# A fused attention and mixture-of-experts kernel on one core: first-layer weights in 8192-byte runs, attention steps ranked for each pair of batches

## The chip, the cores and the metric

The kernel runs on one core of a Trainium2 chip. The metric is the device time of one execution in microseconds (us). Engines are named as in the profile: PE is TensorE's matmul side, PEld its weight loads, DVE VectorE, ACT ScalarE, POOL GpSimd, SP SyncE, which here only issues DMAs. The granted clock (PEclk) is the share of full speed that TensorE's throttle allowed.

## The reference

Two parts, all in float32. The attention has 8 batches, 8 heads, 576 positions, head size 64 and 32 memory slots per head. Its output, laid out as 4608 rows of 512, goes into a softly routed mixture of 8 experts with 4 slots each.

```python
a = exp(phi - max(phi, axis=2)); a = a / (sum(a, axis=2) + 1e-9)      # (8, 8, 576, 32)
k_m = einsum('bhsm,bhsd->bhmd', a, k)                                 # over the 32 memory slots' softmax
v_m = einsum('bhsm,bhsd->bhmd', a, v)
attn = softmax(q @ k_m.T / 8)                                         # over the 32 slots
x = (attn @ v_m), transposed to (4608, 512)

logits = x @ moe_phi                                                  # (4608, 32)
d = softmax(logits, over the 4608 rows);  slot_input = d.T @ x        # (32, 512), 4 rows per expert
for e in range(8):
    slot_out[e] = maximum(slot_input[e] @ w1[e], 0) @ w2[e]           # w1 512x1024, w2 1024x512
out = softmax(logits, over the 32 slots) @ slot_out                   # (4608, 512)
```

q, k and v are 9.4 MB each, phi 4.7 MB, w1 and w2 16.8 MB each, the output 9.4 MB.

## The kernel before, in words

**Staging.** Work goes over four pairs of batches (`bp` 0 to 3, each with `g` 0 and 1) and, inside a pair, over four chunks of two heads (`c`). For a batch, `load_phi`, `load_kv` and `load_q` bring in phi (0.59 MB), k, v and q (1.18 MB each); two buffers each hold phi, the k/v pair and q.
- `shifted`: maximum over positions (DVE, L606), a turn on PE and a second maximum (L614, L621), its copy to all partitions (PE L630, ACT L641), subtraction (POOL, L648), exponential (ACT, L657).
- `summed`: the tree of sums on POOL (four additions, L669), a small product on PE (L679) and a reciprocal on DVE (L688).
- `pooled`: k_m and v_m on PE (L704, 72 products of 64x32 weights, two records each), scaled on the way out by ACT (L721, L728).
- `turned`: transposes of k_m (PE L748, ACT L762) and of v_m (L755, L771), then v_m times moe_phi (L781, L794), so that the logits come straight from the attention weights.
- `turn_q`: 32x32 transposes of q on DVE (L591), two for a batch.
- `scores`, `softmax`, `logits` for a chunk: products (PE L813), transposition out (DVE L827), maximum (L843), subtraction (POOL L848), exponential (ACT L853), sum (DVE L858), reciprocal (L867), multiplication (POOL L871), transposition (DVE L874), logits (PE L882).
- `route`: the softmax over rows within the pair and d.T @ x, through the small pooled forms. Near its end `wtb` is made by a multiply with a mask on DVE (L1065, four blocks of columns of which the mask keeps one per partition), and `sip`, the pair's share of the slots' inputs, by four products on PE (L1085, 8 records).

After the fourth pair the four shares are put together on DVE into SIM (last step L1233). The experts follow: `expert_in` (L1353, w1), `hidden` (L1371, L1380), `expert_out` and `tail_out` (L1413, w2), then the output rows (L1594), their evictions by ACT and DVE (L1570, L1571) and the stores (L1607). `slots` forms the weights of the output (L1523 and around it).

**Order.** Nothing is issued as written. Each step is handed to a planner (`Plan`) with an engine, an assumed cost, what it reads and writes, and a rank. `order` walks through time and takes the step that can begin first on its engine; among those that can begin together, the lowest rank. Ranks come from `plan.at(base, slope)` and, for the attention, from the tables `AT`: one for pair 0, one for pairs 1 and 2, one for pair 3. The nine first loads have a rank of their own, the place of their name in `FIRST`. All loads and stores go through SP's one queue. The planner's DMA rates are constants (`DMA_RATE` for 1 MB loads). Where TensorE has nothing to do at the start, up to `NWARM` warm-up matmuls (L520) are put in.

**Weights.** w1 comes in 16 loads of 1 MB, two for each expert (`load_w`); each puts two rows of 1024 floats (4096 bytes each), 128 rows apart, into a partition. Eleven of w2's 16 halves come in 1 MB loads, with four neighbouring rows of 512 in a partition (8192 bytes in one run); the last five come in 20 quarters of 256 KB, in runs of 1024 bytes, the left half of the output columns first. Weight buffers (`ws`, 2048 floats in each partition) lie over the tiles of the attention and are taken as those are done with.

Of the kernel before, what the change touches and what calls it, by code (L numbers as in the profile page):

```python
# [270 lines left out]
def kernel(  # L271
# [129 lines left out]
    wtbs = stack([2, 2, C, NS], 1)  # L401
# [35 lines left out]
    maskc_b = keep("maskc", [P, C])  # L437
# [6 lines left out]
    NWARM = 40  # L444
# [25 lines left out]
    add(DVE, 3.0, f, r=[ident_b], w=[maskhp_b, maskc_b, rep_b, ones_b])  # L470

# [26 lines left out]
    DMA_RATE, IN_RATE, HALF_RATE, SPREAD = 412e3, 386e3, 350e3, 1.0  # L498
# [8 lines left out]
    FIRST = ["phi0.0", "phi1.0", "mphi", "q0.0", "k0.0", "v0.0", "q1.0", "k1.0", "v1.0"]  # L507
# [37 lines left out]
    class Batch:  # L545
# [146 lines left out]
        def pooled(self, u):  # L692
# [6 lines left out]
            def f(js):  # L699
                for j in js:  # L700
                    for c in range(c0, c1):
                        for a in range(2):
                            h0 = HALF * a
                            nc.tensor.matmul(  # L704
                                acc.ap[M * c: M * c + M, a, : 2 * D],
                                ph()[h0: h0 + HALF, c, j, :],
                                kv()[h0: h0 + HALF, :, c, j * D: j * D + D],
# [5 lines left out]
            for js in (range(0, 3), range(3, 6), range(6, 9)):  # L713
                add(
                    PE, (0.075 * len(js) * self.ks, 8 * len(js) * self.ks), lambda f=f, js=js: f(js),
                    r=[pt.part(u), kvt.part(u), kvt.part(self.units + u)], w=[acc], also=[kp, vm],
                )

            def f():
                for a in range(2):  # L720
                    nc.scalar.activation(  # L721
                        kp.ap[o: o + n].rearrange("p i (r x) -> p i r x", r=R)[:, :, :, HALF * a: HALF * a + Y],
                        acc.ap[o: o + n, a, :D].rearrange("p (i x) -> p i x", i=2).unsqueeze(2)
                        .to_broadcast([n, 2, R, Y]),
                        AF.Copy, scale=rs.ap[o: o + n, a: a + 1],
                    )
                for a in range(2):
                    nc.scalar.activation(  # L728
                        vm.ap[o: o + n, a], acc.ap[o: o + n, a, D: 2 * D], AF.Copy,
                        scale=rs.ap[o: o + n, a: a + 1],  # L730
                    )

            add(
                ACT, 2 * act(P) + 2 * act(D), f, r=[acc, rs.part(u)],
                w=[kp.part(u), vm.part(u)],
            )

        def turned(self, u, vpb):
            kp, vm, kd, vT, n, o, g = self.kp, self.vm, self.kd, self.vT, self.n, u * self.n, self.g
            c0, c1, ks = u * self.ks, u * self.ks + self.ks, self.ks  # L740
            tp, tv, vpp = b_m.tile(), b_m.tile(), b_m.tile()
            ii = ident[o: o + n, o: o + n]

            def f():
                x = tp.ap.rearrange("p (i c r m) -> p i c r m", i=2, c=C, r=R)
                for i in range(2):
# [7 lines left out]
                PE, (TP, 2),  # L754
                lambda: nc.tensor.transpose(  # L755
                    tv.ap[:, :n], vm.ap[o: o + n].rearrange("p a d -> p (a d)"), ii
                ),
                r=[vm.part(u), ident_b], w=[tv], also=[vT],
            )
            add(  # L760
# [6 lines left out]
                r=[tp], w=[kd.part(u)],  # L767
            )
# [225 lines left out]
    def route(bp, ex, pair, lp):  # L994
# [66 lines left out]
        if bp == NSEG - 1:  # L1061
            fill(1, FILL + 5, [wtp])
        add(
            DVE, dve(4 * C * NS),
            lambda: nc.vector.tensor_tensor(  # L1065
                wtb.ap.rearrange("p g a c n -> p (g a) c n"),
                wtp.ap[:, : 4 * NS].rearrange("p (x n) -> p x n", x=4).unsqueeze(2)
                .to_broadcast([P, 4, C, NS]),
                maskc.unsqueeze(1).unsqueeze(3).to_broadcast([P, 4, C, NS]),
                op=ALU.mult,  # L1070
            ),
            r=[wtp, maskc_b], w=[wtb],
# [9 lines left out]
        def f():  # L1082
            for a in range(2):
                for g in range(2):
                    nc.tensor.matmul(  # L1085
                        sip.ap[HALF * a: HALF * a + HALF, :P],
                        pair[g].vm.ap[:, a, :],
                        wtb.ap[:, g, a].rearrange("p c n -> p (c n)"),
                        start=(g == 0),
                        stop=(g == 1),  # L1090
                    )
# [600 lines left out]
```

## Time and profile before

| | |
|---|---|
| runs | 202.66, 202.70 and 220.46 us, median 202.7 |
| profiled execution | 202.39 us, span 200.6 us |
| granted clock, mean | 0.973 |
| bytes moved | 76.47 MB, mean 381 GB/s, 34090 packets |
| packets | 2064 under 512 B, 15888 under 2 KB, 32400 under 8 KB |
| instruction fetches (queue q8) | 20 packets, 0.33 MB |

The prediction quotes the profile. In its slices the span is cut into 40 equal parts of 5 us, and a digit is the busy share in tenths. A row of the view by stretch has, for each engine, busy us and the number of instructions, then the granted clock, the busy share of the 16 DMA engines and GB/s. A timeline row has start and length in us, engine, line, operation, tiles, count, and in brackets the idle time before it and what ended it. A group row has busy us, mean ns of one, then idle time before it and what ended most of that. A row of the waits has total us, number and longest. A row of DMA issues has count, KB each and the median us from issue to landing.

### The profile page before, as it was taken

Reading aid. Unit: us, or ns where it says so; the run is one execution under the profiler, and the core shown is the slowest. Engines: PE = TensorE matmul, PEld = TensorE weight load, DVE = VectorE, ACT = ScalarE, POOL = GpSimd, SP = SyncE. Lnnn points to the kernel's source line nnn. Section 1 sums busy time; section 2 is a strip of 40 time slices with the busy share of each in tenths; the row PEclk is TensorE's granted clock in tenths of the full one; section 3 lists DMA queues with packets and bytes.
Section 4 is the critical chain, followed back from the end, with each engine's and each line's share of the span. In section 5 each row is a group of like instructions: output and inputs, shape, how many; then the busy total and the mean of one; then the engine's idle time right before and its main releaser. Section 6 shows DMA issues by size and latency. Waiting matters only on the chain.

```text
span 200.6 us, 6083 instructions
## 1 busy us (share of the span) xinstructions
PE 172.5 (86%) x2623; PEld 111.0 (55%) x2623; DVE 134.4 (67%) x243; ACT 70.3 (35%) x188; POOL 84.3 (42%) x84
## 2 busy tenths in 40 slices
PE   7999748978699899797999789799999999999930
PEld 6777534636457387464665347464655654557520
DVE  6822640799897899999899996478990110558810
ACT  2022314546341755607463252110201123356600
POOL 7199204589992994889964276000000000000000
PEclk9999997899969999999999999999999999999995
DMA  5999999999999999999999999999999999999996
GB/s 201 362 394 395 381 384 389 381 390 379 397 379 390 389 382 396 383 391 398 404 412 401 409 408 411 408 430 418 415 418 421 378 321 329 356 331 312 398 426 279
DMA packets 34090, 76.47 MB, mean 381 GB/s; under 512 B 2064, under 2 KB 15888, under 8 KB 32400
## 3 DMA queue, kind: packets, MB, share of 16 engines
q1 hardware_dynamic: 34064, 76.09, 100.7%
q8 instruction: 20, 0.33, 0.7%
q14 instruction: 6, 0.05, 0.1%
HBM read 66.65 MB, written 9.44 MB: 379 GB/s over the span
## 4 chain that ended last, share of the span: by engine, by line
PE 34%; DMA 26%; DVE 13%; POOL 11%; issue 4%; SPq 4%; ACT 2%; POOLq 1%; DVEq 0%
DMA arena<-in_moe_w_dram 18%; DMA arena<-in_v_dram 8%; PE bank L1594 6%; PE scbank L813 6%; PE kvbank L704 5%; SPq L502 4%; PE bank L882 4%; POOL arena L848 3%; POOL arena L669 3%; POOL arena L648 3%; POOL arena L871 3%; PE bank L1010 2%; DVE arena L606 2%; DVE arena L827 2%; DVE arena L874 2%
## 5 line engine op out<-in xcount | busy, mean ns | idle before, releaser
L648 POOL TENSOR_TENSOR arena<-arena 128x1152 f32<-128x1152 f32 x8 | 21.0, 2633 | 17.6 <-ACT arena L641 15.1
L591 DVE STREAM_TRANSPOSE arena<-top 128x1152 f32<-128x1152 f32 x16 | 21.6, 1355 | 8.4 <-DMA top<-in_q_dram 8.4
L704 PE MATMUL kvbank<-arena 64*32 64x128 f32 x1152 | 21.2, 279 | 6.1 <-issue 2.9
L520 PE MATMUL kvbank<-ones 128*128 128x256 f32 x82 | 23.7, 426 | 2.4 <-ACT arena L728 1.3
L813 PE MATMUL scbank<-arena 64*64 64x288 f32 x256 | 23.8, 445 | 2.2 <-DVE arena L827 2.1
L669 POOL TENSOR_TENSOR arena<-arena 128x128 f32<-128x128 f32 (+2 forms) x32 | 23.4, 732 | 3.2 <-ACT arena L657 1.3
L704 PEld LDWEIGHTS kvbank<-arena 64*32 64x32 f32 x1152 | 16.5, 107 | 10.8 <-issue 5.9
L871 POOL TENSOR_TENSOR arena<-arena,ssm 128x576 f32<-128x576 f32 x16 | 18.3, 1155 | 9.5 <-DVE ssm L867 7.9
L848 POOL TENSOR_TENSOR arena<-arena,smx 128x576 f32<-128x576 f32 x16 | 18.4, 1153 | 7.6 <-DVE smx L843 7.6
L882 PE MATMUL bank<-arena 128*128 128x288 f32 x64 | 18.8, 425 | 1.3 <-DVE arena L874 0.8
L606 DVE TENSOR_REDUCE arena<-arena 128x128 f32<-128x1152 f32 x8 | 17.1, 2148 | 3.7 <-DMA arena<-in_phi_dram 3.6
L520 PEld LDWEIGHTS kvbank<-ones 128*128 128x128 f32 x82 | 15.9, 209 | 6.1 <-ACT arena L728 1.7
L1571 DVE COPY arena<-bank 128x256 f32<-128x256 f32 (+1 forms) x30 | 14.2, 510 | 5.9 <-PE bank L1594 5.8
L827 DVE STREAM_TRANSPOSE arena<-scbank 128x576 f32<-128x576 f32 x16 | 12.2, 765 | 5.4 <-PE scbank L813 5.4
L1594 PE MATMUL bank<-sr,cT 64*128 64x256 f32 (+1 forms) x104 | 14.7, 355 | 0.7 <-DVE arena L1571 0.6
L813 PEld LDWEIGHTS scbank<-arena 64*64 64x64 f32 x256 | 9.8, 139 | 10.1 <-DVE arena L827 3.6
L853 ACT ACTIVATE arena<-arena 128x576 f32<-128x576 f32 x16 | 11.0, 685 | 11.2 <-POOL arena L848 11.0
L882 PEld LDWEIGHTS bank<-arena 128*128 128x128 f32 x64 | 11.2, 189 | 6.4 <-issue 1.7
L1353 PE MATMUL bank<-arena,SIM 128*32 128x256 f32 x224 | 13.2, 390 | 0.4 <-DVE SIM L1233 0.4
L1594 PEld LDWEIGHTS bank<-sr,cT 64*128 64x128 f32 x104 | 9.9, 185 | 6.4 <-DVE arena L1571 4.6
L1570 ACT COPY arena<-bank 128x256 f32<-128x256 f32 (+1 forms) x24 | 10.3, 445 | 8.4 <-PE bank L1594 7.0
L874 DVE STREAM_TRANSPOSE arena<-arena 128x576 f32<-128x576 f32 x16 | 11.9, 754 | 1.5 <-POOL arena L871 1.5
(139 smaller groups left out, 249.2 us busy)
## 6 DMA issues: line engine op xcount, KB each, us to landing
arena<-in_moe_w_dram SPq DMA_DIRECT2D x25, 1024.0 KB, 14.5
top<-in_q_dram SPq DMA_DIRECT2D x8, 1152.0 KB, 12.6
arena<-in_k_dram SPq DMA_DIRECT2D x8, 1152.0 KB, 10.1
arena<-in_v_dram SPq DMA_DIRECT2D x8, 1152.0 KB, 12.5
arena<-in_moe_w_dram SPq DMA_DIRECT2D x20, 256.0 KB, 6.0
arena<-in_phi_dram SPq DMA_DIRECT2D x8, 576.0 KB, 7.2
out_dram<-arena SPq DMA_DIRECT2D x11, 384.0 KB, 3.4
out_dram<-arena SPq DMA_DIRECT2D x1, 2304.0 KB, 8.1
```

What stands on the lines that cost most here:

```text
L520: lambda: nc.tensor.matmul(warm.ap, ones, ones.unsqueeze(1).to_broadcast([P, 2, P]), start=True, stop=True,),
L591: lambda: nc.vector.transpose(qT.ap.rearrange("p (i u y) -> p u i y", i=2, y=Y), qt.ap[:, h * QT_SZ: h * QT_SZ + QT_SZ].rearrange("p (u i ...
L606: lambda: nc.vector.tensor_reduce(mx.ap[:, c0:c1], ph().rearrange("p c j m -> p c m j"), axis=AX.X, op=ALU.max),
L648: lambda: nc.gpsimd.tensor_tensor(ph(), ph(), mb.ap[:, c0:c1].unsqueeze(2).to_broadcast([P, c1 - c0, J, M]), op=ALU.subtract,),
L669: plus = lambda o, x, y: nc.gpsimd.tensor_tensor(o, x, y, op=ALU.add)
L704: nc.tensor.matmul(acc.ap[M * c: M * c + M, a, : 2 * D], ph()[h0: h0 + HALF, c, j, :], kv()[h0: h0 + HALF, :, c, j * D: j * D + D], start= ...
L813: nc.tensor.matmul(scb.ap[HALF * g: HALF * g + HALF, a, :JY], pair[g].kd.ap[h0: h0 + HALF, i, c].rearrange("p r m -> p (r m)"), pair[g].qT ...
L827: lambda: nc.vector.transpose(ex.ap[:, c * PART: (c + 1) * PART].rearrange("p (a x) -> p a x", a=2), scb.ap[:, :, :JY],),
L848: lambda: nc.gpsimd.tensor_tensor(exv(), exv(), bc(mx), op=ALU.subtract),
L871: lambda: nc.gpsimd.tensor_tensor(exv(), exv(), bc(sm), op=ALU.mult),
L882: nc.tensor.matmul(lp.ap[:, :JY], vpb.ap[:, h, :], aT.ap[:, a * JY: (a + 1) * JY], start=(h == 0), stop=(h == H - 1),)
L1594: nc.tensor.matmul(po.ap[:, : x.stop - x.start], cT[bp].ap[y: y + HALF, j // 2 * P: j // 2 * P + P], sr.ap[y: y + HALF, t, x], start=(t == 0),
```

## The change

Four things are changed together.
1. Each w1 load still brings 256 rows of an expert, but a partition now gets two neighbouring rows, 8192 bytes in one run. The rows are split so that rows 0 to 255 fill partitions 0 to 63 and rows 256 to 511 partitions 64 to 127.
2. For that the slots' inputs must lie in the same order of rows. `wtb` gets two blocks of columns (`i`) in place of four, by a mask `maski` that is the sum of the halves of `maskc`, made once at the start; `sip` is made by 16 products of 64x32 weights with every second column of v_m, in place of four of 128x64. `wtbs` takes 256 floats less in a partition.
3. The first loads come in another order, with two warm-up matmuls fewer, and the planner's rate for 1 MB loads is set from 412 to 419 GB/s.
4. `AT` has a table for each of the four pairs and ranks more steps singly: the maximum, the sums, the softmax of each chunk, the turn of q for each batch, and the v half of what was `turned` (now `turned_k` and `turned_v`). `pooled` can be split in two, for k and for v, but no pair uses it (`if bp in ()`).

```diff
-    wtbs = stack([2, 2, C, NS], 1)
+    wtbs = stack([2, 2, 2, NS], 1)
...
-    maskc_b = keep("maskc", [P, C])
+    maskc_b = keep("maskc", [P, C + 2])
+    maski_b = Tile(ap=maskc_b.ap[:, C:])
...
+    maskc = maskc[:, :C]
-    NWARM = 40
+    NWARM = 38
...
+    add(
+        DVE, 0.1,
+        lambda: nc.vector.tensor_tensor(maski_b.ap, maskc[:, :2], maskc[:, 2:], op=ALU.add),
+        r=[maskc_b], w=[maski_b],
+    )
...
-    DMA_RATE, IN_RATE, HALF_RATE, SPREAD = 412e3, 386e3, 350e3, 1.0
+    DMA_RATE, IN_RATE, HALF_RATE, SPREAD = 419e3, 386e3, 350e3, 1.0
...
-    FIRST = ["phi0.0", "phi1.0", "mphi", "q0.0", "k0.0", "v0.0", "q1.0", "k1.0", "v1.0"]
+    FIRST = [
+        "phi0.0",
+        "v0.0",
+        "k0.0",
+        "q1.0",
+        "v1.0",
+        "phi1.0",
+        "mphi",
+        "q0.0",
+        "k1.0",
+    ]
...
-        def turned(self, u, vpb):
...
+        def turned_k(self, u):
...
+        def turned_v(self, u, vpb):
...
         add(
-            DVE, dve(4 * C * NS),
+            DVE, dve(8 * NS),
             lambda: nc.vector.tensor_tensor(
-                wtb.ap.rearrange("p g a c n -> p (g a) c n"),
+                wtb.ap.rearrange("p g a i n -> p (g a) i n"),
                 wtp.ap[:, : 4 * NS].rearrange("p (x n) -> p x n", x=4).unsqueeze(2)
-                .to_broadcast([P, 4, C, NS]),
-                maskc.unsqueeze(1).unsqueeze(3).to_broadcast([P, 4, C, NS]),
+                .to_broadcast([P, 4, 2, NS]),
+                maski_b.ap.unsqueeze(1).unsqueeze(3).to_broadcast([P, 4, 2, NS]),
                 op=ALU.mult,
             ),
...
         def f():
-            for a in range(2):
+            to = sip.ap[:, :P].rearrange("p (i c n) -> p c i n", i=2, c=2)
+            for c in range(2):
                 for g in range(2):
-                    nc.tensor.matmul(
-                        sip.ap[HALF * a: HALF * a + HALF, :P],
-                        pair[g].vm.ap[:, a, :],
-                        wtb.ap[:, g, a].rearrange("p c n -> p (c n)"),
-                        start=(g == 0),
-                        stop=(g == 1),
-                    )
-
-        add(PE, (0.5, 16), f, r=[wtb, *(x.vm for x in pair)], w=[sip])
+                    for a in range(2):
+                        for y in range(2):
+                            k, x = HALF * y, HALF * y + NS * a
+                            nc.tensor.matmul(
+                                to[x: x + NS, c],
+                                pair[g].vm.ap[k: k + HALF, a, c::2],
+                                wtb.ap[k: k + HALF, g, a],
+                                start=(g == 0),
+                                stop=(g == 1),
+                                tile_position=(k, x),
+                            )
+
+        add(PE, (0.65, 64), f, r=[wtb, *(x.vm for x in pair)], w=[sip])
...
     AT = (
         dict(
...
+            phi=(-1.705, -2.946),
+            max=(-2.707, -6.465),
+            kv=(-0.702, -0.388),
+            sum=(-14.509, 1.214),
+            pool=(-13.306, 6.445),
+            vals=(15.095, 13.191),
+            q=(-2.516, -1.841),
+            turn=(5.179, 26.671, 17.592, 9.626),
+            chunk=(-1.277, -18.958, 1.909, 11.734),
+            soft=(-4.626, -2.857, -0.985, -0.647),
+            logit=(9.329, 4.84, -1.05, 5.792),
+            route=-1.016,
         ),
...
-        at = AT[(bp > 0) + (bp == NBP - 1)]
+        at = AT[bp]
...
+                plan.at(bp + at["max"][i], 8)
                 x.shifted(u)
...
+                plan.at(bp + at["sum"][i], 8)
+                x.summed(u)
                 plan.at(bp + at["pool"][i], 8)
...
+                else:
+                    x.pooled(u)
+                    x.turned_k(u)
+                    plan.at(bp + at["vals"][i], 8)
+                x.turned_v(u, vpb)
...
         for h in range(2):
-            plan.at(bp + at["turn"][h])
             for x in pair:
+                plan.at(bp + at["turn"][2 * h + x.g])
                 x.turn_q(h)
...
             scores(c, pair, ex)
+            plan.at(bp + at["soft"][c], 15)
             aT = softmax(c, ex)
...
-        load(lambda: t.ap.rearrange("p (a x) -> p a x", a=src.shape[1]), src, 1 << 20, t)
+        load(lambda: t.ap, src, 1 << 20, t)
...
-        w1v = w1[e].rearrange("(c p) f -> p c f", p=P)
-        w1b = [load_w(w1v[:, 2 * i: 2 * i + 2], wqs if e == EG else ws) for i in range(2)]
+        w1v = w1[e].rearrange("(y i x z) f -> i y x (z f)", y=2, i=2, z=2)
+        w1b = [load_w(w1v[i], wqs if e == EG else ws) for i in range(2)]
```

More of the change, by code (lines that the diff above doesn't have):

```diff
@@ new lines, in f @@
+                if y1 == 2:
+                    for a in range(2):
+                        nc.scalar.activation(
+                            vm.ap[o: o + n, a], acc.ap[o: o + n, a, D: 2 * D], AF.Copy,
+                            scale=rs.ap[o: o + n, a: a + 1],
+                        )
+            add(
+                ACT, 2 * (1 - y0) * act(P) + 2 * (y1 - 1) * act(D), f, r=[acc, rs.part(u)],
+                w=[kp.part(u), vm.part(u)][y0:y1],
+            )
+        def turned_k(self, u):
+            kp, kd, n, o = self.kp, self.kd, self.n, u * self.n
+            c0, c1 = u * self.ks, u * self.ks + self.ks
+            tp = b_m.tile()
@@ L753, in turned @@
             add(
[L754 to L760, printed above, removed]
                 ACT, act(4 * n),
@@ L767, in turned @@
                 r=[tp], w=[kd.part(u)],
+            )
+        def turned_v(self, u, vpb):
+            vm, vT, n, o, g = self.vm, self.vT, self.n, u * self.n, self.g
+            c0, c1, ks = u * self.ks, u * self.ks + self.ks, self.ks
+            tv, vpp = b_m.tile(), b_m.tile()
+            ii = ident[o: o + n, o: o + n]
+            add(
+                PE, (TP, 2),
+                lambda: nc.tensor.transpose(
+                    tv.ap[:, :n], vm.ap[o: o + n].rearrange("p a d -> p (a d)"), ii
+                ),
+                r=[vm.part(u), ident_b], w=[tv], also=[vT],
             )
@@ new lines @@
+            sum=(-1.871, 1.937),
+            pool=(0.135, -1.398),
+            vals=(-11.982, 8.917),
+            q=(17.271, 14.827),
+            turn=(19.371, 18.133, 6.182, -11.6),
+            chunk=(2.043, 2.611, 4.435, -3.125),
+            soft=(-3.879, -1.92, -13.501, -3.456),
+            logit=(13.98, -5.974, -3.666, -6.149),
+            route=5.225,
+        ),
+        dict(
+            phi=(-10.44, -6.536),
+            max=(1.807, -2.016),
+            kv=(12.416, 7.476),
+            sum=(9.547, -1.136),
+            pool=(-5.739, 1.065),
+            vals=(12.946, 5.088),
+            q=(-5.589, -4.329),
+            turn=(17.511, 18.306, 16.252, 20.8),
+            chunk=(-16.584, -6.307, -19.357, 4.573),
+            soft=(4.398, -14.119, 1.03, -2.376),
+            logit=(-12.129, -16.125, -15.329, -21.346),
+            route=15.794,
```

86 lines of the change are left out of this document (36 added, 50 removed).

## The prediction

> **What bounds the kernel now.** The page comes first: engine shares, then the slices.
>
> ```profile
> PE 172.5 (86%) x2623; PEld 111.0 (55%) x2623; DVE 134.4 (67%) x243; ACT 70.3 (35%) x188; POOL 84.3 (42%) x84
> ...
> DMA  5999999999999999999999999999999999999996
> GB/s 201 362 394 395 381 384 389 381 390 379 397 379 390 389 382 396 383 391 398 404 412 401 409 408 411 408 430 418 415 418 421 378 321 329 356 331 312 398 426 279
> ```
>
> No engine is busy all the time, but the DMA row is 9 from the second slice to the last but one: some transfer is always under way, and what differs is only the rate. The rate follows what is being moved. The view of busy time by stretch shows it:
>
> ```profile
> core 0: us, PE busy (x) PEld busy (x) DVE busy (x) ACT busy (x) POOL busy (x), PEclk, DMA share, GB/s
> 8.00:24.00 16.00, 13.80 (x204) 10.75 (x203) 6.75 (x9) 4.50 (x10) 11.00 (x10) 1.00 1.05 392
> 36.00:96.00 60.00, 52.47 (x1124) 34.46 (x1125) 55.30 (x85) 29.60 (x78) 48.92 (x45) 0.97 1.05 388
> 100.00:130.00 30.00, 26.46 (x277) 16.84 (x266) 25.09 (x45) 11.17 (x36) 13.70 (x13) 1.00 1.03 408
> 132.00:156.00 24.00, 23.33 (x353) 13.92 (x355) 17.04 (x46) 3.97 (x12) 0.00 (x0) 1.00 1.01 418
> 158.00:168.00 10.00, 10.00 (x149) 5.39 (x141) 0.91 (x2) 2.40 (x9) 0.00 (x0) 1.00 1.00 333
> ```
>
> Until about 100 us q, k, v and phi come in, in runs of 2304 and 1152 bytes. The whole 1 MB weight loads follow, first the 16 of w1 (runs of 4096 bytes), then 11 of w2 (8192). From about 157 us the 20 quarter loads run at 333 GB/s. Eleven w2 loads are 11.53 MB, 27.6 us at 418 GB/s, so w2 starts near 129.5: the stretch 100 to 130 is w1, 132 to 156 is w2.
>
> Next, whether TensorE waits for these bytes or the bytes for TensorE. The timeline of TensorE and of its weight loads:
>
> ```profile
> 136.72 7.58 PE L1353 MATMUL bank<-arena,SIM 128*32 128x256 f32 x128 [0.40 <-DVE SIM L1233]
> ...
> 166.96 1.99 PE L1413 MATMUL kvbank<-arena 128*32 128x256 f32 x16
> ...
> 167.59 0.14 PEld L1413 LDWEIGHTS kvbank<-arena 128*32 128x32 f32 x2 [0.47 <-DMA arena<-in_moe_w_dram]
> 168.32 0.15 PEld L1413 LDWEIGHTS kvbank<-arena 128*32 128x32 f32 x6 [0.59 <-DMA arena<-in_moe_w_dram]
> ```
>
> The expert work starts when SIM, the routed sum, is ready (136.4), and then runs almost without a hole. It waits for weights only in the last two groups of the left output half (166.96), 0.47 + 0.59 = 1.06 us. So two chains arrive nearly together at 168.3: the **transfers**, which are last, and the **attention** (through SIM and 32 us of expert matmuls), which is 1.06 us early. Behind that point come output matmuls, evictions and stores, which the change does not touch. So the end moves by the later of: minus the transfer gain, and (SIM's shift minus 1.06).
>
> **The change part by part.** The sum is made against the profiled execution, 202.39 us (span 200.6, 1.79 around it); the median of the three runs is 0.3 above, 202.7.
>
> *w1 in 8192-byte runs.* Bytes and number of loads stay. 16 x 1.0486 = 16.78 MB at 408 GB/s take 41.1 us, at w2's 418 they take 40.1: a gain of 1.0 us if the packet is the whole difference. It needn't be: w1 comes in beside a busy attention part, w2 mostly after it. The loads of q, k, v went at 392 beside a half-idle VectorE (8 to 24) and at 388 beside a full one, 1% less. With that taken from 418, w1 would reach 414 and gain 0.6 us. The ends are 0 and 1.0, and I take 0.8, between the two readings of the w2 row, which is the same kind of load. Total packets should fall by 2048 (16 x 128).
>
> The Trainium skill, "DMA: Bandwidth & Descriptors", section "Why small descriptors are slow (HBM only)", gives a fixed cost of about 3 cycles per packet against one cycle per 32 bytes; by that an estimate for w1 is 413 where w2 has 418, a gain of 0.5 us. The measured 408 is lower than the rule, so here I go by the rows.
>
> *wtb with two instead of four blocks.* The multiply at L1065 shrinks from 512 to 256 columns, and the four sip products become 16 small ones.
>
> ```profile
> L1065 DVE TENSOR_TENSOR arena<-bank,maskc 128x512 f32<-128x512 f32 x4 | 2.7, 672 | 0.8 <-PE bank L1054 0.5 <-ACT arena L1077 0.4
> ...
> L1085 PE MATMUL bank<-arena 128*64 128x128 f32 x32 | 2.7, 285 | 0.3 <-DVE arena L1065 0.3
> ...
> L704 PE MATMUL kvbank<-arena 64*32 64x128 f32 x1152 | 21.2, 279 | 6.1 <-issue 2.9 <-ACT arena L657 2.2 <-DMA arena<-in_v_dram 1.0
> ...
> 136.37 0.29 DVE L1233 TENSOR_TENSOR SIM<-arena 128x128 f32<-128x128 f32 x1
> ```
>
> L1065 takes 672 ns for 512 columns, and L1233 290 ns for 128. The line between gives 417 ns for 256: 0.25 us less, four times 1.0 us of VectorE. On TensorE the 8 records of a sip become 32 of 64x32 shape; the nearest row is L704, 21.2/1152 = 18 ns each, so 0.59 us against 2.7/4 = 0.67: nothing either way. If small products do not overlap at a new tile position, 32 records at w1's expert pace (7.58/128 = 59 ns) are 1.9 us, a loss of 1.2 us at each pair, of which only the last is certainly on SIM's path. The mask add (0.1 to 0.3 us once on VectorE) and two warm-up matmuls fewer fall into the idle start.
>
> *The first loads in another order.* Together they are the same 8.32 MB, so the last one lands at the same time. What runs on them:
>
> ```profile
> 4.68 4.19 DVE L606 TENSOR_REDUCE arena<-arena 128x128 f32<-128x1152 f32 x2 [0.57 <-DMA arena<-in_phi_dram]
> ...
> 16.09 2.24 PE L704 MATMUL kvbank<-arena 64*32 64x128 f32 x144 [0.44 <-DMA arena<-in_v_dram]
> ...
> 25.75 1.94 PE L704 MATMUL kvbank<-arena 64*32 64x128 f32 x116 [0.58 <-DMA arena<-in_v_dram]
> ...
> 27.45 2.08 DVE L606 TENSOR_REDUCE arena<-arena 128x128 f32<-128x1152 f32 x1 [3.03 <-DMA arena<-in_phi_dram]
> ...
> 30.57 0.66 PE L704 MATMUL kvbank<-arena 64*32 64x128 f32 x28 [2.88 <-issue]
> ...
> 31.16 0.33 PE L614 MATMUL bank<-ident,arena 128*128 128x128 f32 x1
> ...
> 31.31 0.63 ACT L721 ACTIVATE arena<-kvbank,prs 128x128 f32<-128x128 f32 x2 [5.36 <-PE kvbank L704]
> ...
> 35.48 1.17 ACT L657 ACTIVATE arena<-arena 128x1152 f32<-128x1152 f32 x1 [1.52 <-POOL arena L648]
> ...
> 35.98 0.79 DVE L827 STREAM_TRANSPOSE arena<-scbank 128x576 f32<-128x576 f32 x1 [4.09 <-PE scbank L813]
> ...
> 38.74 3.17 POOL L669 TENSOR_TENSOR arena<-arena 128x512 f32<-128x512 f32 x4
> ...
> L591 DVE STREAM_TRANSPOSE arena<-top 128x1152 f32<-128x1152 f32 x16 | 21.6, 1355 | 8.4 <-DMA top<-in_q_dram 8.4
> ```
>
> v0 is complete at 16.09 after 4.78 MB, the last load at 25.75 after 8.32: 0.37 MB per us. At that pace phi0, v0 and k0 (2.95 MB) are there at 11.2, and batch 0 pools some 3 us earlier than at 16.09. But phi1 is now sixth: at 5.9 MB it lands at about 19.2 instead of before 6.8. From there: maximum 2.1; then the chain that the third phi shows, from 29.5 (end of its maximum) to 36.65 (end of its exponential), less the 1.6 us that its transpose (31.16) stood behind the stalled matmuls: 5.5. The exponential ends near 26.8, a microsecond after the last k. Pooling 2.2 us ends at 29.0 (31.2 now, with 2.88 us in which TensorE stood still in the middle); the tree of sums, 3.17, ends at 30.0, and with its small matmul and reciprocal L721 comes at about 30.8 (31.31 now). Against this, the first scores, which came at 35.98:
>
> ```profile
> 28.00:32.00 4.00, 0.97 (x31) 0.58 (x31) 1.83 (x2) 0.69 (x3) 0.00 (x0) 1.00 1.05 388
> 32.00:36.00 4.00, 4.00 (x26) 1.97 (x27) 0.02 (x1) 2.00 (x6) 2.62 (x1) 0.59 1.06 380
> ```
>
> Behind four microseconds with TensorE nearly idle the granted clock was 0.59. If the standstill goes, so may this. Between 1 us late (VectorE turns q0 just when phi1 needs it, 1.4 us) and 2 us early I take **1 us early**.
>
> *The steps ranked singly.* A rank only decides between steps that are ready together; it removes no instruction. VectorE is busy 55.30 of 60 us and 25.09 of 30: it sets the pace of the attention, and its idle 9.6 us are all that any order can win there, while a poor one can lose as much. I take nothing. Thus SIM comes some 2 us earlier (1.0 of L1065, 1 of the start), give or take 3 by the order.
>
> *Slots.* SP waits for the two k/v buffers, and these waits can grow:
>
> ```profile
> SPq L502 <- PE kvbank L704: 51.5, 7, 9.8
> ...
> arena<-in_phi_dram SPq DMA_DIRECT2D x8, 576.0 KB, 7.2
> ...
> 0.74 0.98 SPq L502 DMA_DIRECT2D arena<-in_phi_dram  x2
> ```
>
> A phi issued into an empty queue landed after 3.9 us (0.74 to 4.68); the median is 7.2. So about 3.3 us of work still lie in the queue when a slot comes free: the present waits cost nothing, and a pooling later by less than that costs nothing either. The 256 columns that wtb gives up only shift which tiles a weight slot overlaps.
>
> **Sum:** transfers -0.8; SIM -2, so TensorE is early by 1.06 + 2 - 0.8 = 2.3 us and waits for weights. An earlier SIM buys nothing more. 202.39 - 0.8 = 201.6 beside the profile, 201.9 beside the median; I name **201.8**.
>
> **The rivals.**
> 1. *The packets make no difference.* Then 408 is the price of the attention beside it; the pair 392 and 388 speaks for some of that, and for 1% only. The end stays, since TensorE waits for the same last load: 202.5. The Trainium skill, "DMA: Bandwidth & Descriptors", section "Specifications", calls 512 bytes enough for line rate, which would make this the outcome; the rates above, lower with each shorter run (388, 408, 418), speak against it.
> 2. *SIM comes late (the slower side).* The new ranks put gaps into VectorE's work, or the late phi1 and the small sip products delay it. Price: SIM's delay less 1.06 us; it decides once SIM is after 137.5. For 3 us of delay: 202.7 + 1.9 = 204.6. Over 2% slower needs 5.1 us, an 8 us miss of my estimate. For it: 1.06 us is little. Against it: the 2 us above.
> 3. *The DMA runs dry*, when a pooling comes over 3.3 us later than the transfers ask for it: 6 us late would give 202.7 - 0.8 + 2.7 = 204.6, 9 us 207.6. The row of 9s shows no such hole now.
> 4. *More is gained than transfers allow*, through the store part, whose DMA rate dips to 312: at most some 1 us, 200.8.
>
> **How the numbers follow.** Forecast 0.60, rival 1 0.15, rival 2 0.17, rival 3 0.04, rival 4 0.04. Forecast and rivals 1 and 4 lie between 200.8 and 202.7. Rival 2 mostly begins just above; 1 us of its price reaches 203.7, which with rival 3 leaves under 2 in 10 outside. Range 200.7 to 204.0. About 2% (4 us) is what a measurement of this kernel can tell from no change. Faster by more: 0.02, as nothing shown allows 4 us of transfers to vanish; slower by more: 0.05, from the far end of rivals 2 and 3; the rest, 0.93, is within.
>
> **What would show it.** Right: 2048 packets fewer; the w1 stretch at 412 to 418 GB/s; SIM's last step (VectorE's add into SIM) before 136; waits of the L1413 weight loads for DMA of 1 to 4 us; L1065's successor near 0.42 us; batch 1's pooling without its 2.88 us hole. Wrong: a DMA share under 0.9 in any slice before 150 us (rival 3), no DMA waits at L1413 (rival 2), or w1 still at 408 (rival 1).

## The result and the profile after

The changed kernel takes **497.35 us** (median of 4 runs, 495.6 to 498.69) where the kernel before takes 203.19 beside it: 2.449 times as long, interval 2.436 to 2.463. The profiled execution has a span of 496.9 us, against 200.6, and a granted clock of 0.679. The forecast of 201.8 is missed by 296 us, the upper end of its range, 204.0, by 293. In what follows the intervals compare the shorter executions of two kernels; the profiles of e3, e8, e9, e13 and e16 come from executions 1.6 to 3.7% longer than their kernels' shortest, so only totals of them are used, and those of e2 and e15 from executions 1.3 and 1.5% longer.

The page of the changed kernel, engine shares, DMA rows and packets:

```profile
PE 198.2 (40%) x2719; PEld 116.8 (24%) x2719; DVE 134.4 (27%) x244; ACT 69.5 (14%) x188; POOL 84.5 (17%) x84
...
DMA  8999749664611111111111111111111399474998
GB/s 316 375 384 386 228 108 283 254 157 141 216 50 56 55 54 53 55 53 53 53 53 53 52 53 53 53 53 53 55 53 53 131 233 249 177 290 139 297 362 362
DMA packets 31819, 76.49 MB, mean 154 GB/s; under 512 B 1840, under 2 KB 15664, under 8 KB 28080
```

The busy time of the engines is what it was (DVE 134.4 both times; PE has 96 products more and runs at the lower clock). What is new stands in the DMA row: a plateau of 1s from slice 12 to 31 (a slice is 12.4 us), some 248 us at 50 to 56 GB/s. It is neither dry nor full. The stretches give the digit more exactly (columns as in the prediction):

```profile
200.00:240.00 40.00, 4.48 (x40) 1.17 (x32) 0.00 (x0) 0.00 (x0) 0.00 (x0) 0.50 0.13 54
320.00:360.00 40.00, 7.22 (x64) 2.69 (x64) 2.94 (x8) 0.00 (x0) 0.00 (x0) 0.54 0.13 53
460.00:480.00 20.00, 19.64 (x182) 12.59 (x175) 9.79 (x25) 9.04 (x28) 0.00 (x0) 0.96 1.01 323
```

A share of 0.13 is what 2 of 16 engines give (0.125) when both are busy all the time. At 460 to 480, with the quarter loads and the stores, the share is back at 1.01. What is loaded on the plateau is told by SP's queue. On the plateau a single issue lasts 19.3 us:

```profile
44.45 0.69 SPq L509 DMA_DIRECT2D arena<-in_moe_w_dram  x1
...
55.80 0.38 SPq L509 DMA_DIRECT2D arena<-in_phi_dram  x1
...
235.21 19.29 SPq L509 DMA_DIRECT2D top<-in_moe_w_dram  x1
254.54 19.34 SPq L509 DMA_DIRECT2D arena<-in_moe_w_dram  x1
```

One weight load each 19.3 us: 1.0486 MB in 19.34 us is 54 GB/s. The 16 loads of w1 at 53.5 GB/s take 313 us, against 41.1 us before: 272 us more, where the span grew by 296. The waits and the chain show who stood behind them:

```profile
PEld bank L1423 <- DMA arena<-in_moe_w_dram: 159.5, 8, 30.8
PE bank L1423 <- DMA arena<-in_moe_w_dram: 152.9, 8, 30.0
PE bank L1423 <- DMA top<-in_moe_w_dram: 74.7, 2, 37.8
...
DVE arena L623 <- DMA arena<-in_phi_dram: 45.5, 5, 18.7
```

```profile
55.80 25.46 DMA arena<-in_phi_dram
...
100.32 26.47 DMA arena<-in_phi_dram
...
155.15 19.34 SPq L509
```

The expert products (L1423, L1353 before) wait for w1, 153 + 75 us. The attention suffers too: a w1 load issued at 44.45 lies ahead of the phi issued at 55.80, which lands 25.46 us later where the median was 7.2. (In e2 below, where w1 comes at the full rate, a w1 load and this phi are issued at the same times to half a microsecond, 44.46 and 55.45, and the phi lands 5.4 us later.) SIM's last step moves from 136.4 to 176.2 us. That delay is covered by the longer one: the chain goes over to SP's weight loads at 155.

### The profile page after: what moved, and what is told of

It reads as the page before. It is cut to its first block, busy times and chain, and to the rows that moved or that the text cites. A ratio compares the mean times of both kernels' runs of the same rounds, so it can differ in the third digit from the quotient of the medians.

```text
span 496.9 us, 6284 instructions
## 1 busy us (share of the span) xinstructions
PE 198.2 (40%) x2719; PEld 116.8 (24%) x2719; DVE 134.4 (27%) x244; ACT 69.5 (14%) x188; POOL 84.5 (17%) x84
## 2 busy tenths in 40 slices
DMA packets 31819, 76.49 MB, mean 154 GB/s; under 512 B 1840, under 2 KB 15664, under 8 KB 28080
## 4 chain that ended last, share of the span: by engine, by line
SPq 48%; DMA 26%; PE 13%; DVE 6%; POOL 3%; issue 1%; ACT 1%; DVEq 0%; ACTq 0%
SPq L509 48%; DMA arena<-in_phi_dram 14%; DMA arena<-in_moe_w_dram 13%; DVE arena L623 3%; PE bank L1664 3%; PE scbank L841 2%; POOL arena L665 2%; PE bank L910 2%; PE kvbank L1483 1%; PE kvbank L721 1%; PE scbank L1483 1%; PE bank L769 1%; DVE arena L855 1%; PE scbank L1469 1%; DVE arena L608 1%
## 5 line engine op out<-in xcount | busy, mean ns | idle before, releaser
L1423 PE MATMUL bank<-arena,SIM 128*32 128x256 f32 x224 | 22.9, 561 | 153.3 <-DMA arena<-in_moe_w_dram 152.9
L1423 PEld LDWEIGHTS bank<-arena,SIM 128*32 128x32 f32 x224 | 8.3, 144 | 167.2 <-DMA arena<-in_moe_w_dram 159.5
L1423 PE MATMUL bank<-top,SIM 128*32 128x256 f32 x32 | 3.9, 629 | 74.7 <-DMA top<-in_moe_w_dram 74.7
L841 PE MATMUL scbank<-arena 64*64 64x288 f32 x256 | 24.9, 488 | 2.9 <-DVE arena L855 2.9
L910 PE MATMUL bank<-arena 128*128 128x288 f32 x64 | 20.9, 461 | 1.1 <-DVE arena L902 1.1
L1423 PEld LDWEIGHTS bank<-top,SIM 128*32 128x32 f32 x32 | 1.2, 156 | 76.9 <-issue 39.5
L1581 DVE CAST cS<-L 128x288 fp32r<-128x288 f32 x4 | 1.8, 452 | 63.3 <-PE bank L1423 37.3
L631 PE MATMUL bank<-ident,arena 128*128 128x128 f32 x8 | 2.9, 358 | 38.1 <-DVE arena L623 38.1
L1483 PE MATMUL kvbank<-arena 128*32 128x256 f32 x128 | 13.6, 511 | 8.5 <-DMA arena<-in_moe_w_dram 8.3
```

The lines of the kernel that those rows point to most:

```text
L841: nc.tensor.matmul(scb.ap[HALF * g: HALF * g + HALF, a, :JY], pair[g].kd.ap[h0: h0 + HALF, i, c].rearrange("p r m -> p (r m)"), pair[g].qT ...
L910: nc.tensor.matmul(lp.ap[:, :JY], vpb.ap[:, h, :], aT.ap[:, a * JY: (a + 1) * JY], start=(h == 0), stop=(h == H - 1),)
L1423: nc.tensor.matmul(hb.ap[NS * j: NS * j + NS, :256], SIM.ap[:, 2 * i + c, NS * e: NS * e + NS], wv[:, c, 512 * (j // 2): 512 * (j // 2) + ...
L1483: nc.tensor.matmul(dst[NS * x: NS * x + NS, :HD], hT()[:, 4 * k + 2 * i + j, NS * e: NS * e + NS], wide[:, j, k, d * HD: d * HD + HD], sta ...
```

## The experiments

The theory after this trace (A): the number of DMA engines of a load follows the outermost count of its DRAM pattern. The new pattern `i y x (z f)` has `y`, 2, in that place; the old one, `p c f`, has 128. Rivals: the way in which DRAM is read (B), or the new ranks starving the queue (C). The kernels e2, e4, e5, e7, e12 and e14 bring w1's rows in another order than the slots' inputs have and leave that matching out; the work is of the same size.

### e4 and e5: the outermost count by itself

e4 is the kernel before, ranks and 4096-byte runs included, with only the order of w1's pattern changed:

```diff
-        w1v = w1[e].rearrange("(c p) f -> p c f", p=P)
-        w1b = [load_w(w1v[:, 2 * i: 2 * i + 2], wqs if e == EG else ws) for i in range(2)]
+        w1v = w1[e].rearrange("(y w x) f -> w y x f", y=2, w=4)
+        w1b = [load_w(w1v[2 * i: 2 * i + 2], wqs if e == EG else ws) for i in range(2)]
...
+            load(lambda z=z: t.ap[:, FF * z: FF * z + FF], src[z], 1 << 19, t.part(z))
```

> The kernel before, its ranks too, but each w1 load is two DMAs of 512 KB whose DRAM pattern has an outermost count of 2 (two ranges of 64 rows, 1 MB apart), with runs of 4096 bytes as before. Leaves out the right order of w1's rows. Theory A: again 53 GB/s and a DMA share of 0.13 while w1 comes in, 470 to 520 us. Theory B with 8192-byte runs as the cause: 202 to 206 us. Theory B with the 1 MB step: slow, as theory A. Theory C: 202 to 206 us.

Measured: 497.45 us in one run, the time of the changed kernel, and the same stretch:

```profile
320.00:360.00 40.00, 4.32 (x32) 0.81 (x32) 0.00 (x0) 0.00 (x0) 0.00 (x0) 0.50 0.13 53
```

The 8192-byte runs and the ranks are not needed for it: B (for the long runs) and C fall. What is left of B is the jump of 1 MB between two ranges of rows, which e4 has too. e5 is the changed kernel with one number altered, an outermost count of 4:

```diff
-        w1v = w1[e].rearrange("(y i x z) f -> i y x (z f)", y=2, i=2, z=2)
+        w1v = w1[e].rearrange("(y i x z) f -> i y x (z f)", y=4, i=2, z=2)
```

> The changed kernel with w1's rows cut into four ranges instead of two, so that the DRAM pattern's outermost count is 4 (32 partitions each); still one DMA of 1 MB with 8192-byte runs. Leaves out the matching order of the slots' inputs. Theory A (a load uses as many of the 16 DMA engines as its outermost count): 4/16, DMA share 0.25 and 107 GB/s while w1 comes in alone, w1 takes 157 us instead of 313, total 330 to 350 us. Theory E (any pattern that jumps between ranges of rows is slow, whatever their number): near 497 us, or worse.

Measured: 352.49 us.

```profile
200.00:240.00 40.00, 7.98 (x70) 3.15 (x74) 4.45 (x13) 0.00 (x0) 0.00 (x0) 0.54 0.25 106
```

Counts of 2, 4 and 128 give shares of 0.13, 0.25 and 1.0 and 53, 106 and 408 to 418 GB/s: some 26.5 GB/s an engine. The time is just above A's 330 to 350; E, for which any jump between ranges is slow, falls, since four ranges are faster than two.

The count can also be read without any rate, in the packets under 512 B. e11 below has 16 loads more than the kernel before, all over 128 partitions, and 256 such packets more (2320 against 2064): 16 for a load. Pages of e11, e4 and e5:

```profile
DMA packets 34346, 76.47 MB, mean 367 GB/s; under 512 B 2320, under 2 KB 16144, under 8 KB 32656
DMA packets 33898, 76.47 MB, mean 154 GB/s; under 512 B 1872, under 2 KB 15696, under 8 KB 32208
DMA packets 31851, 76.49 MB, mean 218 GB/s; under 512 B 1872, under 2 KB 15696, under 8 KB 28112
```

The changed kernel has 1840, 224 fewer than before: 14 fewer for each of its 16 w1 loads, so 2 are left. e4 has 448 fewer than e11 with as many loads, 14 for each of 32; e5 192 fewer than the kernel before, 12 for each of 16, so 4 are left.

### e1, e12, e14, e11: the same rows in several loads

e1 leaves the rows as the change has them and issues each w1 load as two of 64 partitions, so that 64 is outermost:

```diff
-        load(lambda: t.ap, src, 1 << 20, t)
+            for y in range(2):
+                load(lambda y=y: t.ap[HALF * y: HALF * y + HALF], src[y], 1 << 19, t.part(y))
```

> The changed kernel, but each 1 MB load of w1 goes out as two DMAs of 512 KB, one for partitions 0 to 63 and one for 64 to 127. Same addresses, same 8192-byte runs, same ranks. Theory A (a load is spread over as many of the 16 DMA engines as the outermost count of its DRAM pattern allows; that count is 2 in the changed kernel, hence a DMA share of 0.13 and 53 GB/s): the outermost count becomes 64, w1 runs at 400 to 418 GB/s, DMA share near 1 throughout, 200.5 to 203 us. Theory B (w1 is slow because of what is read: 8192-byte runs, or the two ranges of rows 1 MB apart): the same bytes stay slow, 400 to 500 us. Theory C (the new ranks starve the queue): about 497 us, unchanged.

Measured: 250.43 us, 1.232 (1.225 to 1.239).

```profile
150.00:160.00 10.00, 6.48 (x51) 4.63 (x51) 5.50 (x11) 1.57 (x5) 4.79 (x5) 0.71 1.02 234
```

All 16 engines are busy, as A says, but they move 234 GB/s, not some 400. The addresses are those of the changed kernel, so the jump of 1 MB, the rest of B, falls as well. Is it the smaller load, or the partitions it fills? e11 cuts the loads of the kernel before in two of 512 KB, each over all 128 partitions; e12 has four of 32 partitions; e14 has three, of partitions 0 to 31, 32 to 95 and 96 to 127.

```diff
 e11 (kernel before)
+        for z in range(2):
+            load(lambda z=z: t.ap[:, FF * z: FF * z + FF], src[:, z], 1 << 19, t.part(z))
 e12 (changed kernel, y=4)
+            for y in range(4):
+                load(lambda y=y: t.ap[NS * y: NS * y + NS], src[y], 1 << 18, t.part(y))
 e14 (changed kernel, w1 as "(i p z) f -> i p (z f)")
+        for y, (a, b) in enumerate(((0, 32), (32, 96), (96, 128))):
+            load(lambda a=a, b=b: t.ap[a:b], src[a:b], (b - a) << 13, t.part(y))
```

> The kernel before, but each 1 MB load of w1 goes out as two DMAs of 512 KB that both fill all 128 partitions (runs of 4096 bytes, outermost count 128). Theory H (the two DMAs for 64 partitions each ran at 234 GB/s because a DMA into half of the partitions moves at half the rate): w1 at 400 to 412 GB/s, 202 to 205 us. Rival I (512 KB DMAs cost a fixed 1 us more each): w1 near 234 GB/s, 240 us or more.

> The changed kernel with each 1 MB load of w1 as four DMAs of 256 KB, each for 32 partitions (outermost count 32 in each, runs of 8192 bytes). Leaves out the matching order of the slots' inputs. Theory H: a quarter of the rate, 115 to 120 GB/s with a DMA share near 1, w1 takes 140 to 145 us, total 310 to 340 us. Rival I: 1 MB takes 4 x (0.63 + 1.0) = 6.5 us, 160 GB/s, total 270 to 290 us.

> The changed kernel with each 1 MB load of w1 as three DMAs, for partitions 0 to 31, 32 to 95 and 96 to 127 (256, 512 and 256 KB, runs of 8192 bytes). Leaves out the matching order of the slots' inputs. Theory K (partitions 0 to 63 are reached through one half of the ports into the on-chip memory, 64 to 127 through the other, so any DMA within one half moves at half the rate): the 512 KB in the middle at 418 GB/s, the two others at 234, on average 300 GB/s or more while w1 comes in alone. Theory L (a DMA with fewer than 128 partitions is slow, whichever they are): 234 GB/s throughout, as with the halves and the quarters.

Measured: e11 210.13, e12 244.47, e14 238.7 us, one run each. Stretches of w1 of e11, then e12, then e14:

```profile
120.00:130.00 10.00, 8.77 (x106) 4.95 (x104) 9.32 (x17) 3.91 (x12) 6.03 (x6) 1.00 1.02 408
```

```profile
140.00:150.00 10.00, 10.00 (x144) 7.46 (x143) 5.99 (x21) 1.69 (x7) 0.00 (x0) 1.00 1.00 229
```

```profile
110.00:120.00 10.00, 7.11 (x127) 5.27 (x122) 9.59 (x15) 4.22 (x16) 5.32 (x5) 1.00 1.02 256
...
150.00:160.00 10.00, 10.00 (x176) 5.79 (x170) 9.45 (x27) 2.11 (x5) 0.00 (x0) 1.00 1.01 231
```

The size is not it: 512 KB over 128 partitions go at 408 (e11 is slower in total because the planner, given twice as many loads, orders the attention otherwise; SIM comes at 145.3). A quarter of the partitions is hardly slower than half, 229 beside 234, and neither theory's time for e12 came. The Trainium skill, "SBUF — State Buffer", section "Door 1: The DMA port swizzle", says that partitions 0 to 63 reach 8 of 16 ports, and 0 to 31 the same 8. e1 and e12 agree. By it e14's middle load, half of the bytes, should reach all 16: an estimate of 0.52 MB at 418 and 0.52 MB at 234, 3.5 us for 1.05 MB, is 300 GB/s. e14's stretches show 231 to 256, nearer to theory L's 234 (fewer than 128 partitions are slow, whichever they are) than to the estimate. So the rule isn't borne out for that load, and whether the ports are the whole cause stays open.

### e7: the 8192-byte runs alone

The kernel before, with only the rows of w1 changed; order and ranks are the same, instruction for instruction:

```diff
-        w1v = w1[e].rearrange("(c p) f -> p c f", p=P)
-        w1b = [load_w(w1v[:, 2 * i: 2 * i + 2], wqs if e == EG else ws) for i in range(2)]
+        w1v = w1[e].rearrange("(i p z) f -> i p (z f)", i=2, z=2)
+        w1b = [load_w(w1v[i], wqs if e == EG else ws) for i in range(2)]
```

> The kernel before with nothing changed but w1's runs: partition p of half i gets rows 256i + 2p and 2p + 1, one DMA of 1 MB, outermost count 128. Leaves out the matching order of the slots' inputs. The order of all instructions is that of before. The recorded term (packets): 408 GB/s between 100 and 130 us become 414 to 418, the waits of the w2 products for weights shrink from 1.06 us to 0 to 0.5, total 0.6 to 1.0 us less, 201.6 to 202.0. Rival (408 is the price of the attention beside it): still 405 to 410 GB/s, 202.6. SIM at 136.4 by both, which caps the gain at 1.06 us.

Measured: 201.65 us, 0.9958 (0.9937 to 0.9979), 0.85 us less. The stretches of w1 and w2, and the last wait for weights:

```profile
100.00:130.00 30.00, 26.04 (x275) 16.45 (x260) 24.67 (x44) 11.28 (x36) 13.54 (x12) 1.00 1.01 416
132.00:156.00 24.00, 23.34 (x351) 13.52 (x351) 16.81 (x46) 3.83 (x11) 0.00 (x0) 1.00 1.01 418
```

```profile
PEld kvbank L1413 <- DMA arena<-in_moe_w_dram: 0.2, 1, 0.2
```

The rate goes from 408 to 416, and TensorE's wait at the end from 1.1 to 0.2 us. The packet was nearly the whole of the difference between w1 and w2; rival 1 falls.

### e2 and e3: the rest of the change

e2 is the changed kernel, all of it, with 128 outermost:

```diff
-        w1v = w1[e].rearrange("(y i x z) f -> i y x (z f)", y=2, i=2, z=2)
+        w1v = w1[e].rearrange("(i p z) f -> i p (z f)", i=2, z=2)
```

> The changed kernel, but partition p of half i gets rows 256i + 2p and 2p + 1, so that one DMA of 1 MB has an outermost count of 128. Leaves out the matching order of the slots' inputs (rows of w1 meet the wrong inputs); operations and sizes are the same. Theory A: w1 at 412 to 420 GB/s, 200.5 to 203 us, and if 512 KB pieces cost anything, 0.3 to 1 us faster than the halves. Theory B with 8192-byte runs as the cause: 400 to 500 us. Theory B with the 1 MB step as the cause: as theory A. Theory C: about 497 us.

Measured: 203.62 us, 1.0027 (0.9991 to 1.0063), no change. The pattern of w1's loads makes the 294 us. Its timelines of VectorE and of TensorE answer the small terms of the sum:

```profile
34.53 0.78 DVE L855 STREAM_TRANSPOSE arena<-scbank 128x576 f32<-128x576 f32 x1 [4.00 <-PE scbank L841]
...
80.35 0.42 DVE L1093 TENSOR_TENSOR arena<-bank,maskc 128x256 f32<-128x256 f32 x1 [1.31 <-ACT arena L1105]
...
138.98 0.29 DVE L1303 TENSOR_TENSOR SIM<-arena 128x128 f32<-128x128 f32 x1
```

```profile
26.02 1.94 PE L721 MATMUL kvbank<-arena 64*32 64x128 f32 x118 [1.02 <-issue]
28.28 0.65 PE L721 MATMUL kvbank<-arena 64*32 64x128 f32 x26 [0.31 <-issue]
```

Its stretches at 54 to 58 us:

```profile
54.00:56.00 2.00, 1.54 (x41) 1.29 (x42) 0.33 (x2) 0.38 (x1) 0.00 (x0) 1.00 0.82 334
56.00:58.00 2.00, 2.00 (x12) 1.23 (x11) 1.97 (x4) 1.66 (x7) 0.39 (x1) 1.00 0.74 195
```

The first scores come 1.45 us earlier (35.98 before), the smaller multiply takes 0.42 us, but SIM comes at 139.0, 2.6 us later. And the transfers run dry for a moment. SP's queue in the kernel before, then in e2:

```profile
52.63 0.37 SPq L502 DMA_DIRECT2D arena<-in_phi_dram  x1
```

```profile
55.45 0.37 SPq L509 DMA_DIRECT2D arena<-in_phi_dram  x1
```

The same phi is issued 2.8 us later, and the share falls to 0.82 and 0.74.

e3 has the new tables of ranks, first loads, warm-ups and planner's rate, and w1, mask and `sip` as before:

```diff
-    NWARM = 40
+    NWARM = 38
...
-    DMA_RATE, IN_RATE, HALF_RATE, SPREAD = 412e3, 386e3, 350e3, 1.0
+    DMA_RATE, IN_RATE, HALF_RATE, SPREAD = 419e3, 386e3, 350e3, 1.0
...
-        at = AT[(bp > 0) + (bp == NBP - 1)]
+        at = AT[bp]
```

> Only the ranks, the order of the first loads, the warm-up count and the planner's rate are new; w1's rows, the mask multiply and the sip products are those of before (runs of 4096 bytes, outermost count 128). Theories A and B: w1 at 408 GB/s and near the kernel before, 201 to 204.5 us, with SIM's last step between 134 and 139 us (by the recorded estimate 1 us earlier than 136.4, without the 1 us of the smaller multiply). Theory C: far slower, 400 us or more.

Measured: 211.84 us (207.99 to 212.17). Even the shortest is 5.4 above the kernel before, and outside every theory: A and B had at most 204.5, C 400 or more. The new order without the smaller multiply and the finer `sip` costs more than the whole of e2. Perhaps these ranks fit only the costs of the kernel that has the rest of the change; that is not shown.

### e8, e9, e10, e13: the long runs with the rows in their right order

Can the 0.85 us of e7 be had? e8 is the kernel before with e7's rows and 16 products for `sip` of 128x32 weights; e9 the same under the new ranks (the changed kernel with w1 as in e2, `wtb` of four blocks, and e8's products).

```diff
+            to = sip.ap[:, :P].rearrange("p (y c n) -> p y c n", y=2, c=2)
+            for c in range(2):
...
+                                to[x: x + NS, :, c],
+                                pair[g].vm.ap[:, a, c::2],
+                                wtb.ap[:, g, a, i::2],
...
-        add(PE, (0.5, 16), f, r=[wtb, *(x.vm for x in pair)], w=[sip])
+        add(PE, (0.65, 64), f, r=[wtb, *(x.vm for x in pair)], w=[sip])
```

> The kernel before with 8192-byte runs of w1 (outermost count 128) and the slots' inputs in the matching order: sip by 16 products of 128x32 weights and 64 columns in place of 4 of 128x64 weights and 128 columns, the mask multiply as before. Ranks, first loads and the planner's rate as before. If the new ranks are what made SIM late: SIM at 136 to 137.5, total as with the rows alone or up to 0.5 us more, 201.6 to 202.5. If the finer sip is what made it late: SIM after 138, 203 or more.

> As the run before (8192-byte runs, the same 16 sip products, the old mask multiply), but with the new ranks, order of first loads, warm-up count and planner's rate. If the new ranks make SIM late: SIM at 138 or later, 203 to 212 us. If the two-block multiply and its sip made it late: SIM near 136, 201.5 to 202.5.

Measured: e8 215.24 us, 1.0599 (1.0550 to 1.0648); e9 212.88, 1.0305 (1.0242 to 1.0368). By these expectations both the ranks and the finer `sip` would be at fault, and e8 is slower by twelve microseconds. Two kernels part the causes: e13 is the kernel before with only the planner's number changed (the last two lines of the diff), e10 is e8 with the old number, so with the order of before.

> The kernel before with one number changed: the planner is told that sip takes 0.65 us and 64 instructions instead of 0.5 and 16. Every instruction is that of before, w1's loads too; only the order of steps changes, to that of the run of 215 us. Theory F: 210 to 218 us, SIM after 145. Rival G: 202 to 203.5 us, SIM near 136.4.

> 8192-byte runs of w1 with an outermost count of 128 and the 16 finer sip products, as in the run that took 215 us with the old ranks, but the planner is told the old cost of sip (0.5 us, 16 instructions), so that all steps stand in the order of before. Theory F (the order that the planner makes is what the late SIM comes from; the finer sip itself costs nothing): SIM at 136.4 to 137.5, 201.5 to 202.3 us, ratio 0.995 to 0.999. Rival G (the finer products themselves delay the attention): SIM after 140, 206 us or more.

Measured: e13 214.6 us, 1.0589 (1.0572 to 1.0605); e10 206.04, 1.0169 (1.0155 to 1.0182). **The order alone costs 12 us**: a step's assumed 0.65 us and 64 records in place of 0.5 and 16, and no instruction changed. e10 keeps 3.5 us that the order doesn't explain. TensorE's timeline of e7, then of e10:

```profile
73.92 0.66 PE L1085 MATMUL bank<-arena 128*64 128x128 f32 x8
74.41 0.63 PE L781 MATMUL bank<-mphd,arena 128*64 128x64 f32 x8
...
75.28 0.94 PE L704 MATMUL kvbank<-arena 64*32 64x128 f32 x48
...
77.27 2.21 PE L882 MATMUL bank<-arena 128*128 128x288 f32 x8
```

```profile
74.13 0.66 PE L1089 MATMUL bank<-arena 128*32 128x64 f32 x32
74.72 0.68 PE L781 MATMUL bank<-mphd,arena 128*64 128x64 f32 x8
...
75.64 0.90 PE L704 MATMUL kvbank<-arena 64*32 64x128 f32 x45
78.59 0.41 PE L704 MATMUL kvbank<-arena 64*32 64x128 f32 x3 [2.05 <-issue]
...
80.06 3.90 PE L882 MATMUL bank<-arena 128*128 128x288 f32 x8
```

The 32 small records take the same 0.66 us as the 8 large ones. The loss begins with a stop of 2.05 us three products before the end of a pooling, with nothing in the view that it waited for. The logits behind it start 2.8 us later and end 4.5 later: they take 3.90 us in place of 2.21, at a lower granted clock (e10, then e7):

```profile
80.00:84.00 4.00, 4.00 (x14) 2.87 (x11) 1.57 (x3) 0.22 (x2) 2.26 (x2) 0.57 0.94 320
80.00:84.00 4.00, 3.52 (x34) 2.20 (x32) 3.82 (x5) 2.50 (x6) 4.00 (x3) 1.00 1.06 383
```

SIM, at 141.1, is 4.4 after e7's 136.7. So F is right on e13 and wrong on e10, where G's forecast came (SIM after 140, 206 us or more): the finer products are all that parts e10 from e7. They delay the attention, but not by their own length.

### e15 and e16: where the stops fall

If such a stop belongs to a place in the list of instructions, fewer records ahead of it should move it. e15 and e16 are e10 without the last 6 and 12 of the warm-ups that are placed, so with 24 and 48 records fewer (weight loads counted). e15's edit; e16 has 19 for 25:

```diff
-                lambda: nc.tensor.matmul(
+                lambda k=k: None if n == NWARM and k >= 25 else nc.tensor.matmul(
```

> The repaired kernel in the order of before (206 us), with the last 6 of the warm-up matmuls that TensorE runs left out: 24 records fewer before the first sip product, all else in the same order. Theory J (its loss is the stop of 2.05 us at 76.5 us, inside the pooling, where TensorE waits for its next block of instructions, and the slow logits behind it, 3.90 us in place of 2.21): the stop moves or goes, SIM somewhere between 136 and 143, the total changes by 1 us or more either way. Rival M (the finer products cost it): SIM at 141, 206 us as before.

> The same with 12 warm-up matmuls fewer: 48 records, just as many as the first pair's finer sip adds, so that between 75 and 110 us the blocks of instructions end at the steps where they ended with the rows alone (201.65 us). Theory J: no stop near 76.5 us, SIM at 136.5 to 139.5, 201.7 to 204 us, unless a new stop appears before 75 us. Rival M: SIM at 141, 206 us.

Measured: e15 206.89 us, 1.0114 (1.0023 to 1.0205); e16 207.86, 1.0248 (1.0209 to 1.0287). In e15's timeline the stop stands a microsecond later, in another step:

```profile
79.77 0.76 PE L813 MATMUL scbank<-arena 64*64 64x288 f32 x7 [2.29 <-issue]
```

Neither theory's total came: e15's executions lie anywhere between 203.34 and 208.96 and decide nothing, and all of e16's are above both J's 204 and M's 206. But J's place is right to the record. In e10 three products of the pooling are left when TensorE stops; in e15 these three and nine of the scores' 16 have run, and 12 products with their 12 weight loads are the 24 records left out. Counted from the start, the place is the same in e10, e15 and e2, whose order is another. Each has run 1240 products shortly before the stop ends:

```profile
0.00:78.50 78.50, 64.39 (x1240) 44.76 (x1240) 54.43 (x82) 30.04 (x74) 51.83 (x55) 0.96 1.03 375
0.00:79.70 79.70, 64.23 (x1240) 45.14 (x1240) 54.42 (x82) 31.23 (x79) 51.81 (x55) 0.91 1.03 375
0.00:82.90 82.90, 68.32 (x1240) 46.68 (x1240) 57.24 (x90) 31.20 (x80) 54.23 (x57) 0.92 1.01 367
```

The DMA view of narrow windows has more: each of these stops ends 2.4 to 2.6 us after an instruction fetch (queue q8) began, which was at 76.1, 77.3 and 80.4 us (ends 78.59, 79.77 and 83.01). So does the stop of 2.88 us in the kernel before (fetch at 28.1, end 30.57). e7 has its 1240 products behind it at 78.6 us, 2.7 after the fetch at 75.8, and runs through. So the count of records sets where TensorE can be stopped, and it is stopped if it gets there too soon after the fetch began. A wait for the fetched instructions fits all of these; no run varies the fetches by themselves, so this cause is read from the traces and not tested. The planner reckons with such places, in blocks of 256 TensorE instructions (`BLOCK`), and takes the number of a step's instructions from the same entry that e13 alters. In e10 that entry is too low, 16 for 64.

## Why the prediction was wrong

**The step that failed** is the first of the change: "Bytes and number of loads stay", with the ends 0 and 1.0 us and the choice 0.8. I priced the length of the runs as the only thing that the new pattern changes, and bounded the cost by rows of loads that all have 128 partitions outermost. The pattern's outermost count went from 128 to 2, and with it the engines from 16 to 2: 272 us in place of -0.8. e5 shows it by the count, e4 without any other part of the change, e2 by taking it away. The Trainium skill has the rule, and I missed it: "DMA: Bandwidth & Descriptors", section "Why a DMA increments its semaphore by 16 and not by 1", lets a DMA use the largest number up to 16 that divides the sizes of the slowest dimensions of both patterns. The trace agrees: 2 gives 0.13, 4 gives 0.25. No rival had it either: I had none on the new pattern being slower than the old. A load pattern that the trace of before doesn't show has no upper bound in rows of other patterns.

**Terms that held**, by e2 and e7, where the loads use all engines. The runs: 0.8 forecast, 0.85 measured, at 416 GB/s (412 to 418 forecast). Packets: 2048 fewer forecast; e2 has 32043 against 34090, 2047 fewer with one instruction fetch more. The multiply: 417 ns forecast, 0.42 us. `sip`'s 32 records: 0.59 us forecast, 0.58 in e2's chain. The first scores: 1 us early forecast, 1.45 measured; of batch 1's stop of 2.88 us 0.31 is left (the 1.02 in front of the pooling ends as k1 lands, at 25.9). That term came out partly by luck: phi1 landed at 15.7 us where I had 19.2, and its exponential ended at 24.1, not 26.8, so that the last k, and not phi1, set the pooling's start.

**Terms that were mis-sized**, hidden under the 290 us in the changed kernel itself. "I take nothing" for the ranks: SIM was to be 2 us earlier and is 2.6 later in e2's profile, so 4.6 us were lost on the way, though the start and the multiply gained what they were to gain. That is rival 2, and its price, 2.6 less 1.06, 1.5 us, is near e2's span (202.5 against 200.6); its sign shows too, as the weight loads of L1413 (L1483 here) wait only 0.2 us. But its reasons, gaps in VectorE's work, a late phi1 and the `sip` products, are not the larger part. Three of the stops described above stand in e2's chain:

```profile
53.31 1.15 issue
...
75.81 0.73 issue
...
81.14 1.86 issue
```

They are 3.7 of the 4.6 us; the chain of the kernel before has no such piece above 0.61 us between 31 and 122 us. (The miss that rival 2 needs for 2% is 5.1 + 2 = 7.1 us, not the 8 that I wrote.) My bound for an order, the 9.6 us that VectorE idles, was too narrow for a loss: e13 loses 12 by order alone. "About 3.3 us of work still lie in the queue": an issue 2.8 us late already left a gap, so the cushion there was smaller. Against 388 GB/s, e2 lacks 2 us x 54 and 2 us x 193 GB/s at 54 to 58, 0.49 MB or 1.3 us, which leaves a cushion of about 1.5. So rival 3's hole is there, small, beside rival 2. In the changed kernel itself the sign that I named for it, a share under 0.9 before 150 us, came from the slow loads, and those weight loads waited 13.3 us for w2, where 1 to 4 were named.

## To carry to other kernels

For each load whose access pattern changes, read off the outermost count of the DRAM side before pricing anything else; on this chip's traces a DMA share that stands still at c/16 (0.13, 0.25) names the count c. Keep all 128 partitions in one load: loads of 32 and 64 partitions went at 229 to 256 GB/s here, where whole ones have 408 to 418. Count TensorE's records when a step is split: in e10, 48 more moved a stop into a pooling and SIM came 4.4 us later, though the products took no longer. An order that was searched for belongs to the costs that it was searched with: one entry, 0.65 us and 64 records for 0.5 and 16, moved the end by 12 us, so a change of costs and a change of ranks are to be measured apart and together.

## What was not expected of the hardware

- A load keeps as many DMA engines busy as its outermost count (2, 4, or all 16 for 32, 64 and 128); an engine moves some 26.5 GB/s where the load fills all partitions. A load on two engines holds up others issued behind it: phi took 25 to 26 us instead of 7.2.
- Loads that fill 32 or 64 partitions go at 229 to 236 GB/s with all 16 engines busy, against 408 to 418, and a load of partitions 32 to 95 among them didn't bring the rate over 256.
- TensorE stands still for up to 2.88 us without a wait in the list of waits, at fixed counts of its products (1240 in e10, e15 and e2), and goes on 2.4 to 2.6 us after an instruction fetch began. e7 comes to the same count later and doesn't stop.
- Behind such a stop the granted clock was 0.57 for 4 us in e10, where e7 had 1.00.
